# RWKV attention and MLP in one kernel: w spread by a product, the last two tiles turned on TensorE, a new order

## The chip, the cores and the metric

The kernel runs on one core of one Trainium2 chip. The metric is the device time of one execution in microseconds, given as the median of several runs. A core has five engines with a queue of instructions each: TensorE (PE in the profile, with its weight loads as PEld), VectorE (DVE), ScalarE (ACT), GpSimd (POOL) and SyncE (SP), which here only issues DMAs. ACT issues DMAs too. Products of PE land in PSUM and are taken out by DVE or ACT.

## The reference

A recurrence with decay over 768 steps for 4 batches and 8 heads of 48, then a layer norm, a two-layer MLP with relu, and a residual:

```python
for t in range(S):
    cur = np.einsum('bhd,bhe->bhde', u[None] * kt, vt)
    y[:, :, t] = np.einsum('bhd,bhde->bhe', rt, state + cur)
    state = w[None, :, :, None] * state + np.einsum('bhd,bhe->bhde', kt, vt)
...
xn = (x - mu) / np.sqrt(var + 1e-06) * g_ln
ch = np.maximum(xn @ w_ch1, 0.0) @ w_ch2
return x + ch
```

x is y with the heads side by side: 3072 rows of 384. The MLP is 384 to 1536 to 384. Inputs and output are fp32.

## The kernel before

The rows are cut into 24 tiles of 128 steps (tile i is chunk i // 4 of batch i % 4). For each tile, r and k are scaled by powers of w (`SR`, `SK` with the factors `Fr`, `Fk`), turned so that the head dimension lies on partitions (`TR` on PE with copies `TCr`, `TCk`, `TC`; from tile 12 on `TKR`, a DMA transpose issued by SP, into `trs`), multiplied (`Q`), and made into score products (`AT`, masked by `AM` into `A`). `S` makes the state update and the u term in a PSUM bank named s, `CC` and `ZU`/`ZS`/`ZD` take them out, `Y` makes the tile's output in the same bank, and `X` adds the u term `Vb` and sums the row. `CV` casts v to bf16. `SQ`, `XN` and `RS` are the layer norm. xn is then turned again: for the early tiles by `LT` on PE with a copy `XT`, for pairs by `LT2` and for the last four tiles by `LTD`, both DMA transposes on SP, into `xT`.

The MLP goes by groups of one or two tiles (`GROUPS`): `UP` (PE, 12 or 6 products into one of two banks hp), `RL` (relu to bf16 `hT`, ACT or DVE), `DN` (PE, four products each into bank o), `OT` (DVE, scale and residual into one of four slots of `ot`) and `STO` (store). The last tile's output is made in two halves.

Weights come in three slabs for each layer (`LW1`, `LW2`, into the same buffers `w1_f`). `SW` scales each part of a first-layer slab by the layer norm's weight and casts it, `CW` casts the second layer's. The loads of k, r and v (`LK`, `LR`, `LV`) are 192 KB each.

At the start w is loaded to all 128 partitions (`WF`), `LN` takes its logarithm, `FK` and `FR` make the factors. `DU` puts products on a tile of zeros into PSUM that nobody reads (an argument of 8 is two of 512 columns).

Nothing is scheduled by a tool: `PLAN` is a list of steps, each with an index and an engine (s, v, g for ACT, DVE, POOL), and every engine runs its steps in the order of this list. SP carries all loads, the DMA transposes and most stores in one queue, so an issue that waits holds up all that stand behind it.

Of the kernel before, what the change touches and what calls it, by code (L numbers as in the profile page):

```python
# [7 lines left out]
FP32 = mybir.dt.float32  # L8
# [10 lines left out]
WF,0,s LK,0,- MP,0,v MM,0,g LR,0,- MI,0,g MW,0,v LK,1,- LC,0,s DU,8,- TL,0,s DU,16,- LR,1,- LC,1,s DU,48,- LV,0,- LN,0,s LC,2,s FK,0,s LR,2,- FR,0,s  # L19
SK,0,v LK,2,- SR,0,v SK,1,v TR,0,- LV,1,- SR,1,g CT,0,- TCk,0,v DU,8,- LK,3,- CP,0,v CV,0,s UW,0,g TR,1,- TCr,0,s LR,3,- SR,2,v TCk,1,s AT,0,- Q,0,v  # L20
WL,0,s DU,8,- LV,2,- TCr,1,v SK,2,g S,0,- AMb,0,v DU,8,- CC,0,s LV,3,- Q,1,v TR,2,- CV,1,s VB,0,g ZU,0,v DU,8,- TCk,2,s LW1,0,- AMa,0,v S,1,- SK,3,g
TCr,2,s LW1,2,- CC,1,v ZU,1,v AT,1,- UGC,0,s DU,8,- Q,2,g LK,4,- AMa,1,v Y,0,- AT,2,- X,0,v LR,4,- CV,2,g AMa,2,v S,2,- SR,3,g DU,8,- AMb,1,v CC,2,s
CV,3,v VB,1,g TR,3,- ZU,2,v LR,5,- AMb,2,v TCr,3,s Y,1,- XN,0,g DU,8,- SQ,0,s X,1,v DU,8,- TCk,3,s Y,2,- XN,1,g SW,1,s Q,3,v RS,0,g LT,1,- SW,0,v
DU,8,- XT,1,s SW,2,v DU,8,- VB,2,v LT,0,- UP,16,- XT,0,s LV,4,- SW,7,v SW,6,s AT,3,- X,2,v UP,0,- LK,5,- SK,4,v S,3,- RL,16,v RL,0,s LW1,1,- SR,4,g
SW,8,v XN,2,s LR,6,- CC,3,v AM,3,v UP,2,- VB,3,g LK,6,- TR,4,- SR,5,g ZU,3,v UP,18,- TC,4,s LK,7,- LT,2,- SK,5,v Y,3,- RL,2,s Q,4,v TR,5,- X,3,v
DU,8,- CV,4,v XN,3,s S,4,- XT,2,v TC,5,v LR,7,- UP,32,- SW,3,s SW,4,g SW,5,v RL,18,s ATP,4,- Q,5,g ZU,4,v RL,32,s UP,17,- AM,4,v LV,5,- SR,6,g UP,1,-
RL,17,s LV,6,- CC,4,s SQ,1,s RL,1,v Y,4,- VB,4,g UP,33,- SQ,2,s AM,5,v LW2,1,- SK,6,g LT,3,- DU,8,- LW2,0,- XT,3,v TR,6,- LW2,2,- X,4,v DU,2,- UP,49,-
TC,6,s RL,33,v LV,7,- CV,5,v S,5,- SK,7,v SR,7,v UP,50,- ZU,5,v TR,7,- CC,5,v XN,4,v Q,6,v TC,7,s LR,8,- LT,4,- CV,6,v S,6,- RL,50,v XT,4,s Q,7,g
RL,49,s CC,6,v ZU,6,v ATP,6,- CW,3,s UP,34,- VB,5,g AM,6,v CW,2,s Y,5,- RS,2,g LK,9,- DN,5,- CW,0,s CW,1,v RS,1,g X,5,v UP,48,- RL,34,s VB,6,v XN,5,s
Y,6,- DN,4,- RL,48,s X,6,v LR,9,- CW,4,s LT,5,- CW,5,v UP,66,- XN,6,g AM,7,v SQ,3,s DN,6,- UP,64,- LK,11,- OT,1,v CV,7,s S,7,- LK,8,- SR,8,g DN,2,-  # L30
CC,7,s ZU,7,v DN,0,- LR,10,- RL,66,s XT,5,v SK,9,v Y,7,- RL,64,s LV,9,- DN,1,- SR,9,v SQ,5,s VB,7,v UP,80,- LV,8,- OT,0,v TR,9,- X,7,v LR,11,- UP,65,-
SK,8,g TC,9,s DN,8,- LK,10,- RL,65,s Q,9,v TR,8,- SR,10,v RL,80,s LV,10,- DN,10,- CV,9,g XN,7,v SQ,4,s DN,9,- TC,8,s CV,8,g LT2,6,- S,9,- RS,4,g
OT,2,v UP,81,- Q,8,v SR,11,g ATP,8,- LK,12,- ZU,9,v RL,81,s UP,82,- CC,9,v STO,0,s AM,8,v LK,13,- S,8,- SK,10,g RL,82,s DN,18,- LR,12,- ZU,8,v CC,8,s
DN,17,- VB,9,g AM,9,v Y,8,- VB,8,g TR,10,- LV,11,- SK,11,v UP,96,- TC,10,s ZD,8,g X,8,v DN,16,- LV,12,- RL,96,s UP,98,- Q,10,g CV,10,s LR,13,- TR,11,-
XN,8,s Y,9,- SQ,6,s TC,11,v RS,5,g LK,15,- UP,97,- RL,98,s OT,4,v SK,12,g ATP,10,- STO,1,- SQ,7,s X,9,v DN,21,- RL,97,s Q,11,v SR,12,g XN,9,s S,10,-
UP,100,- ZU,10,v RS,3,g TKR,12,- DN,20,- AM,10,v RL,100,s DN,22,- CC,10,s CV,12,s VB,10,g AM,11,v SQ,8,s LV,14,- Y,10,- UP,101,- CV,11,g LT2,8,-
SR,13,g OT,5,v UP,99,- X,10,v DN,13,- LV,13,- RL,99,s ZD,10,v LR,14,- S,11,- RL,101,s ZD,9,v DN,12,- SK,13,v DN,14,- ZU,11,v TKR,13,- UP,112,- Q,12,v
CC,11,v VB,11,v Y,11,- RL,112,s STO,2,- OT,3,v UP,117,- CV,13,v UP,115,- STO,3,- X,11,v SR,14,g LK,14,- DN,29,- XN,11,s LV,15,- Q,13,v RS,6,g S,12,-
RL,117,s ATP,12,- ZU,12,v CC,12,s DN,28,- XN,10,v RL,115,s AM,12,v VB,12,g LT2,10,- DN,30,- ZD,11,g UP,116,- OT,7,v LR,15,- Y,12,- AM,13,v RL,116,s
LK,17,- UP,113,- STO,4,- DN,24,- X,12,v RL,113,s LR,16,- DN,25,- ZD,12,v SK,14,v S,13,- UP,114,- SK,15,v TKR,14,- CC,13,v ZU,13,v UP,133,- VB,13,g  # L40
RL,114,s SR,15,v Y,13,- RL,133,s UP,132,- X,13,v TKR,15,- UP,128,- RL,132,v SR,16,g DN,26,- RL,128,s LK,16,- UP,131,- SQ,9,s OT,6,v CV,14,g LR,17,-
XN,12,s UP,129,- Q,14,v RS,7,g XN,13,s S,14,- DN,32,- CV,15,s ZU,14,v LT2,12,- Q,15,g SQ,13,s ATP,14,- CC,14,v VB,14,v RL,131,s DN,33,- SK,16,g
# [23 lines left out]
def kernel(  # L66
# [12 lines left out]
    nc = tc.nc  # L79
# [87 lines left out]
    w_p = cols[:, :HP]  # L167
# [52 lines left out]
    def MW(i, e):  # L220
        nc.vector.memset(rows[:], 1.0)
        nc.vector.memset(warm[:], 0.0)  # L222
# [433 lines left out]
```

## Time and profile before

| | us |
|---|---|
| median of three runs | 155.81 (155.64 to 156.53) |
| profiled execution | 154.18 |
| its span, first to last instruction | 152.4 |
| PE busy, of it unread products | 141.2, 13.6 |
| DVE, ACT, POOL busy | 113.8, 78.2, 77.7 |
| first up product, first output product | 20.36, 39.67 |

Busy times are unions of an engine's instructions, with the tail of the product pipeline; a product's own mean duration is therefore longer than the distance between two of them. "Idle before" with an arrow names what ended an engine's wait. The chain of waits, followed back from the end, runs mostly over PE (57% of the span) and SP's queue (14%).

### The profile page before, as it was taken

The numbers are of one execution on the slowest core, as the hardware profiler recorded it, in microseconds if no ns is written. First come the engines' busy times: TensorE is split into PE (matmuls) and PEld (weight loads), VectorE is DVE, ScalarE is ACT, GpSimd is POOL, SyncE is SP. The second block draws the span as 40 slices with busy tenths as digits, with TensorE's granted clock in tenths as the row PEclk, the third lists the DMA queues.
The fourth block names the chain that finished last, engine by engine and source line by source line (L and its number), as shares of the span: only waits on it lengthen the run. The fifth ranks groups of instructions, "written<-read, shape, count | busy, mean of one in ns | idle before, by whom it ended". The sixth has DMA issues, their size and how long they took to land.

```text
span 152.4 us, 4296 instructions
## 1 busy us (share of the span) xinstructions
PE 141.2 (93%) x1716; PEld 108.6 (71%) x1716; DVE 113.8 (75%) x238; ACT 78.2 (51%) x169; POOL 77.7 (51%) x115
## 2 busy tenths in 40 slices
PE   4998897899899999999997999799999999999991
PEld 1365477686778878877885788577886776878871
DVE  2449889989777995896976989699869965743521
ACT  1555465666957739635359384411962152934020
POOL 3058836571743979915328948067404909450100
PEclk9999999999999999999999999999999999999999
DMA  3999989999889989689999899988998997133122
GB/s 76 200 230 202 361 180 247 233 232 395 242 165 200 199 197 215 143 174 256 121 228 207 159 216 208 206 172 205 211 217 179 229 200 175 58 96 117 49 103 103
DMA packets 100241, 28.98 MB, mean 190 GB/s; under 512 B 95355, under 2 KB 98686, under 8 KB 100222
## 3 DMA queue, kind: packets, MB, share of 16 engines
q1 hardware_dynamic: 98752, 26.94, 81.0%
q10 hardware_dynamic: 1470, 1.77, 3.4%
q8 instruction: 13, 0.21, 0.6%
q14 instruction: 6, 0.05, 0.1%
HBM read 19.08 MB, written 4.72 MB: 156 GB/s over the span
## 4 chain that ended last, share of the span: by engine, by line
PE 57%; SPq 14%; DMA 11%; POOL 5%; ACT 5%; DVE 3%; issue 3%; POOLq 0%; DVEq 0%; ACTq 0%
PE o L550 23%; PE hp L520 22%; SPq L322 6%; DMA trs<-sc 4%; SPq L319 4%; DMA w_f<-in_moe_w_ch_dram 4%; DMA out_dram<-ot 3%; SPq L325 3%; PE s L437 2%; POOL q L190 2%; PE s L445 2%; PE at L341 2%; PE at L364 2%; POOL sc L190 1%; PE s L408 1%
## 5 line engine op out<-in xcount | busy, mean ns | idle before, releaser
L520 PE MATMUL hp<-xT,w_sb 128*128 128x128 bf16 (+1 forms) x612 | 57.1, 242 | 1.6 <-DVE hT L538 0.6
L550 PE MATMUL o<-w_sb,hT 128*128 128x384 bf16 x276 | 52.2, 326 | 1.5 <-DVE ot L608 1.1
L520 PEld LDWEIGHTS <-w_sb 128*128 128x128 bf16 x612 | 48.6, 114 | 5.6 <-issue 0.7
L536 ACT ACTIVATE hT<-hp 128x512 bf16<-128x512 f32 x56 | 32.9, 597 | 34.4 <-PE hp L520 33.9
L550 PEld LDWEIGHTS <-hT 128*128 128x128 bf16 x276 | 25.1, 97 | 14.5 <-issue 1.7
L374 DVE TENSOR_TENSOR A<-at,mask 128x1024 bf16<-128x1024 f32 (+1 forms) x27 | 29.1, 1094 | 0.0
L608 DVE SCALAR_TENSOR_TENSOR ot<-o,rs,x 128x384 f32<-128x384 f32 x23 | 14.1, 614 | 10.6 <-PE o L550 8.3
L190 POOL TENSOR_TENSOR sc<-rf,Fr 128x384 bf16<-128x384 f32 x12 | 12.4, 1034 | 16.7 <-DMA rf<-in_r_dram 16.7
L427 POOL TENSOR_TENSOR Vb<-vf,cc 128x384 f32<-128x384 f32 x16 | 13.6, 851 | 11.0 <-DVE cc L187 9.6
L257 PE MATMUL o<-warm 128*128 128x512 bf16 x42 | 13.6, 456 | 2.0 <-DVE warm L222 2.0
L452 DVE SCALAR_TENSOR_TENSOR x<-s,Vb 128x384 f32<-128x384 f32 x24 | 13.2, 550 | 2.3 <-PE s L445 1.6
L459 ACT ACTIVATE sqj<-x,sm 128x384 bf16<-128x384 f32 x24 | 14.7, 614 | 0.0
L190 POOL TENSOR_TENSOR q<-trs 128x512 bf16<-128x512 bf16 x8 | 9.2, 1153 | 8.8 <-DMA trs<-sc 4.6
L185 ACT COPY trs<-at 128x512 bf16<-128x512 bf16 (+1 forms) x12 | 9.5, 798 | 8.1 <-PE at L341 6.9
L538 DVE TENSOR_SCALAR hT<-hp 128x512 bf16<-128x512 f32 x16 | 10.8, 685 | 2.5 <-PE hp L520 2.5
L190 DVE TENSOR_TENSOR q<-trs 128x512 bf16<-128x512 bf16 x16 | 8.1, 509 | 4.7 <-DMA trs<-sc 3.3
L190 POOL TENSOR_TENSOR sc<-kf,Fk 128x384 bf16<-128x384 f32 x9 | 9.7, 1082 | 3.8 <-PE o L550 3.2
L190 DVE TENSOR_TENSOR sc<-kf,Fk 128x384 bf16<-128x384 f32 x15 | 8.4, 562 | 4.2 <-ACT Fk L270 4.0
L476 POOL TENSOR_TENSOR rs<-rs,expo 128x1 f32<-128x1 f32 (+1 forms) x17 | 10.7, 632 | 1.4
L465 ACT ACTIVATE xn<-x,sm 128x384 bf16<-128x384 f32 x13 | 7.9, 615 | 5.6 <-DVE x L452 5.6
L473 POOL TENSOR_SCALAR rs<-sq 128x1 f32<-128x1 f32 (+1 forms) x17 | 4.1, 244 | 12.7 <-ACT sqj L459 11.7
L395 PEld LDWEIGHTS <-q 128*128 128x128 bf16 x96 | 5.5, 97 | 4.9 <-DVE q L190 1.3
(75 smaller groups left out, 172.4 us busy)
## 6 DMA issues: line engine op xcount, KB each, us to landing
kf<-in_k_dram SPq DMA_DIRECT2D x24, 192.0 KB, 4.0
rf<-in_r_dram SPq DMA_DIRECT2D x24, 192.0 KB, 3.9
vf<-in_v_dram SPq DMA_DIRECT2D x24, 192.0 KB, 3.8
w_f<-in_moe_w_ch_dram SPq DMA_DIRECT2D x6, 768.0 KB, 7.8
out_dram<-ot SPq DMA_DIRECT2D x16, 192.0 KB, 2.2
out_dram<-ot ACTq DMA_DIRECT2D x7, 192.0 KB, 2.2
w_all<-in_w_dram ACTq DMA_DIRECT2D x1, 192.0 KB, 3.9
trs<-sc SPq DMA_TRANSPOSE x12, 3.6
```

The costliest lines, as they stand in the source:

```text
L190: engines[e].tensor_tensor(out=out, in0=in0, in1=in1, op=ALU.mult)
L257: nc.tensor.matmul(out=warm_ps[0][:], lhsT=warm[:], rhs=warm[:].unsqueeze(1).to_broadcast([P, 4, P]), start=True, stop=True)
L374: nc.vector.tensor_tensor(out=AA(i)[:, a:b].rearrange("p e q t -> p (e q) t"), in0=psum["at", i][:, a:b].rearrange("p e q t -> p (e q) t") ...
L427: engines[e].tensor_tensor(out=Vb(i)[:].rearrange("p (h d) -> p h d", h=H), in0=vf(i)[:], in1=cc(i)[:].unsqueeze(2).to_broadcast([P, H, D] ...
L452: nc.vector.scalar_tensor_tensor(out=xx(i)[:], in0=psum["y", i][:, :C], scalar=1.0, in1=Vb(i)[:], op0=ALU.mult, op1=ALU.add, accum_out=sm[ ...
L459: nc.scalar.activation(out=sqj[:], in_=xx(i)[:], func=ACT.Square, bias=sm[i][:], scale=-float(C), accum_out=sq[g][:, j : j + 1])
L476: nc.gpsimd.tensor_tensor(out=rs[g][:], in0=rs[g][:], in1=expo[:, :n], op=ALU.pow)
L520: nc.tensor.matmul(out=t[:, a * gw : (a + 1) * gw].rearrange("p (j t) -> p j t", j=size), lhsT=w1_sb[n][kc][:, fb::FB], rhs=xT(g)[:, :size ...
L536: nc.scalar.activation(out=o, in_=s, func=ACT.Relu)
L538: nc.vector.tensor_relu(out=o, in_=s)
L550: nc.tensor.matmul(out=psum["o", i][:, :C], lhsT=hT(g)[:, fk, j * P : (j + 1) * P], rhs=w2_sb[d][:, a, :], start=(seen == 0 and a == 0), s ...
L608: nc.vector.scalar_tensor_tensor(out=ot(i), in0=psum["o", i][:, :C], scalar=rs[g][:, j : j + 1], in1=xx(i)[:], op0=ALU.mult, op1=ALU.add,)
```

## The change

Three edits of the code, and a new `PLAN`. w is loaded as one row; a product of a row of ones with it spreads it to 128 partitions in PSUM, in fp32, and `LN` reads it there. The last two tiles' xn is turned by `LT` and `XT` where it was `LTD`. The unread products go from 42 wide and 2 narrow ones to 4 wide ones.

```diff
-    w_all = const.tile([P, H, D], FP32, name="w_all")
+    w_row = const.tile([1, H * D], FP32, name="w_row")
+    one = const.tile([1, P], FP32, name="one")
...
     def WF(i, e):
         issuer(e).dma_start(
-            out=w_all[:].rearrange("p h d -> p (h d)"), in_=w.rearrange("h d -> (h d)").partition_broadcast(P)
+            out=w_row[:], in_=w.rearrange("h d -> (h d)").rearrange("(o x) -> o x", o=1)
         )
...
+        nc.vector.memset(one[:], 1.0)
...
+    def WB(i, e):
+        t = psum["w"] = ps.tile([P, 512], FP32, name="s")
+        nc.tensor.matmul(out=t[:, :C], lhsT=one[:], rhs=w_row[:], start=True, stop=True)
+
     def LN(i, e):
-        nc.scalar.activation(out=ln_all[:], in_=w_all[:], func=ACT.Ln)
+        nc.scalar.activation(
+            out=ln_all[:].rearrange("p h d -> p (h d)"), in_=psum["w"][:, :C], func=ACT.Ln
+        )
...
-WF,0,s LK,0,- MP,0,v MM,0,g LR,0,- MI,0,g MW,0,v LK,1,- LC,0,s DU,8,- TL,0,s DU,16,- LR,1,- LC,1,s DU,48,- LV,0,- LN,0,s LC,2,s FK,0,s LR,2,- FR,0,s
+WF,0,s LR,0,- MP,0,v MI,0,g LK,0,- MW,0,v LC,0,s LC,1,- WB,0,- TL,0,s LV,0,- DU,8,- LR,1,- LK,1,- LC,2,s LN,0,s FR,0,s LR,2,- FK,0,s SR,0,v LK,2,-
```

The sums over engines move too: ACT does 7 fewer casts and scalings of weights, v and xn, POOL 5 more casts of v, 4 more scalings of weights and 5 more scalings of k and r; SP issues 18 full stores where it issued 16.

The first place is SP's queue where the first-layer weight slabs (w1_f) are loaded among tiles of k, r and v (the digit behind kf, rf, vf is the tile). Before:

```order
L319 DMA kf3_72<-in_k_dram 128x8x48
L322 DMA rf3_83<-in_r_dram 128x8x48
L325 DMA vf2_93<-in_v_dram 128x8x48
L325 DMA vf3_94<-in_v_dram 128x8x48
L294 DMA w1_f0_231<-in_moe_w_ch1_dram 128x3x512
L294 DMA w1_f2_233<-in_moe_w_ch1_dram 128x3x512
L319 DMA kf4_73<-in_k_dram 128x8x48
L322 DMA rf4_84<-in_r_dram 128x8x48
L322 DMA rf5_85<-in_r_dram 128x8x48
L325 DMA vf4_95<-in_v_dram 128x8x48
L319 DMA kf5_74<-in_k_dram 128x8x48
L294 DMA w1_f1_232<-in_moe_w_ch1_dram 128x3x512
```

The same place of the changed kernel, after nine rows of tiles 0 to 4:

```order
L332 DMA vf1_92<-in_v_dram 128x8x48
L329 DMA rf3_83<-in_r_dram 128x8x48
L326 DMA kf5_74<-in_k_dram 128x8x48
L326 DMA kf3_72<-in_k_dram 128x8x48
L301 DMA w1_f0_232<-in_moe_w_ch1_dram 128x3x512
L332 DMA vf2_93<-in_v_dram 128x8x48
L326 DMA kf4_73<-in_k_dram 128x8x48
L301 DMA w1_f1_233<-in_moe_w_ch1_dram 128x3x512
L332 DMA vf3_94<-in_v_dram 128x8x48
L329 DMA rf5_85<-in_r_dram 128x8x48
L301 DMA w1_f2_234<-in_moe_w_ch1_dram 128x3x512
```

vf2 and vf3 have moved behind the first and the second slab, and the third slab has come forward past vf4. On PE the first up product (`UP,0`) now stands behind the state products of tile 3 (`S,3`), which read vf3; before, two `UP` stood ahead of `S,3`.

The second place is POOL's queue around the scalings of the first-layer weights (w1_sb, L305 before and L312 now). Before:

```order
L473 TENSOR_SCALAR rs0_198<-sq0_180 128x1
L476 TENSOR_TENSOR rs0_198<-rs0_198,expo_218 128x1
L190 TENSOR_TENSOR sc1_103<-rf4_84,Fr_220 128x8x48
L427 TENSOR_TENSOR Vb0_128<-vf3_94,cc3_119 128x384
L190 TENSOR_TENSOR sc2_104<-rf5_85,Fr_220 128x8x48
L305 TENSOR_SCALAR w1_sb1_1_238<-w1_f1_232,g_neg_228 128x512
L190 TENSOR_TENSOR q1_113<-trs2_111 128x512
```

Now:

```order
L434 TENSOR_TENSOR Vb2_130<-vf2_93,cc2_118 128x384
L312 TENSOR_SCALAR w1_sb0_1_236<-w1_f0_232,g_neg_229 128x512
L312 TENSOR_SCALAR w1_sb1_0_238<-w1_f1_233,g_neg_229 128x512
L190 TENSOR_TENSOR sc2_104<-rf5_85,Fr_220 128x8x48
L312 TENSOR_SCALAR w1_sb1_2_240<-w1_f1_233,g_neg_229 128x512
L312 TENSOR_SCALAR w1_sb2_2_243<-w1_f2_234,g_neg_229 128x512
L187 CAST vv2_107<-vf6_97 128x384
L312 TENSOR_SCALAR w1_sb2_0_241<-w1_f2_234,g_neg_229 128x512
L190 TENSOR_TENSOR sc0_102<-rf6_86,Fr_220 128x8x48
```

POOL scaled one part of nine before and scales five now, with the cast of vf6 between the third slab's two parts.

More of the change, by code (lines that the diff above doesn't have):

```diff
@@ new lines @@
+LV,6,- SW,3,g X,2,v CV,3,s LT,1,- SK,5,v XN,2,s LK,6,- S,3,- AM,3,v SR,5,g SQ,1,s UP,0,- SW,5,g XT,1,v ZU,3,v UP,16,- CC,3,v VB,3,v LT,2,- SW,4,v
+TR,5,- RL,16,s XT,2,v Y,3,- RL,0,s LK,7,- DU,8,- SW,8,g X,3,v UP,33,- Q,4,v LV,5,- CV,4,s XN,3,v S,4,- TC,5,s SW,7,v LR,7,- CV,6,g LT,3,- UP,32,-
+XT,3,v RL,33,s SW,6,g Q,5,v LR,6,- ATP,4,- RL,32,s SK,6,v UP,34,- LW2,0,- AM,4,v UP,18,- LW2,1,- RL,34,s CC,4,v UP,17,- RL,18,s ZU,4,v VB,4,v LW2,2,-
+Y,4,- RL,17,s CV,5,v UP,1,- SR,7,v LV,7,- UP,50,- RL,1,s X,4,v SR,6,g AM,5,v SQ,4,s S,5,- SQ,2,s RS,1,g LR,9,- TR,6,- ZU,5,v RL,50,s UP,2,- RS,0,g
@@ new lines @@
+SK,13,g DN,20,- SK,12,v SR,13,g Y,10,- OT,5,v TKR,12,- UP,96,- X,10,v DN,14,- RS,3,g AM,11,v XN,10,s TKR,13,- DN,12,- CV,11,g RL,98,s DN,13,- SQ,8,s
+Q,11,v SR,14,v LK,14,- S,11,- RL,96,s OT,3,v UP,117,- LV,14,- ZD,9,v DN,28,- STO,3,- RL,117,s CC,11,v CV,13,v VB,11,g UP,112,- ZU,11,v LR,15,- CV,12,s
+Q,12,v Y,11,- ZD,10,g LV,15,- RL,112,s UP,113,- X,11,v SQ,9,s UP,115,- Q,13,g SQ,11,s ATP,12,- STO,4,- RL,115,v XN,11,s S,12,- SK,14,g STO,2,-
+RL,113,s AM,12,v DN,29,- LT2,10,- DN,30,- CV,14,g CC,12,v ZU,12,v SK,15,g UP,116,- OT,7,v TKR,14,- Y,12,- VB,12,v SR,15,g DN,25,- X,12,v DN,24,-
@@ new lines @@
+VB,15,v UP,146,- LR,18,- OT,9,v UP,147,- LK,19,- RL,146,s DN,42,- CV,16,s RL,147,v Q,16,g DN,41,- X,15,v UP,145,- XN,14,v XN,15,s S,16,- RL,145,s
+LT2,14,- DN,40,- ZU,16,v SQ,13,s UP,144,- OT,10,v LV,17,- UP,149,- SK,18,v RL,144,s STO,9,- CC,16,v Q,17,v ATP,16,- VB,16,g RL,149,s LR,19,- DN,46,-
+STO,7,s AM,16,v LV,18,- SR,18,g SQ,14,s DN,45,- UP,163,- AM,17,v RS,9,g TKR,18,- Y,16,- RL,163,s CV,17,g UP,161,- ZD,15,v SK,19,g LR,21,- UP,165,-
+X,16,v RL,161,s DN,44,- RL,165,s SR,19,v S,17,- XN,16,s UP,148,- TKR,19,- CC,17,v OT,11,v VB,17,g UP,162,- ZU,17,v RL,148,s ZD,16,v Q,18,g DN,52,-
@@ new lines @@
+LV,19,- CV,18,s SQ,15,s LK,21,- Y,17,- DN,53,- X,17,v SR,21,g UP,160,- RL,162,v XN,17,s S,18,- RS,10,g RL,160,s LT2,16,- DN,54,- ZU,18,v SQ,17,s
+ATP,18,- CC,18,v OT,13,v VB,18,g SQ,16,s STO,8,- UP,164,- ZD,17,v ZD,18,g LR,20,- DN,48,- AM,18,v RL,164,s LK,20,- DN,50,- STO,10,- SK,21,g AM,19,v
+DN,49,- Y,18,- UP,177,- OT,12,v TKR,21,- X,18,v UP,181,- RL,177,s Q,19,v DN,56,- CV,19,s STO,11,- SK,20,v S,19,- LK,23,- DN,58,- CC,19,s ZU,19,v
+RL,181,s LK,22,- DN,57,- SR,20,v UP,179,- TKR,20,- OT,14,v Y,19,- Q,21,v RL,179,s DN,60,- VB,19,v LR,22,- XN,18,v UP,178,- X,19,v LV,20,- UP,180,-
@@ L62 @@
+DN,90,- RL,256,s DN,88,- STO,21,s DN,89,- DB,1,- OT,22,v DB,0,- DB,2,- STO,22,- DA,1,- OB,23,v DA,0,- SB,23,- DA,2,- OA,23,v SA,23,s
 """
@@ L617 @@
     steps = dict(
-        WF=WF, LC=LC, CT=CT, CP=CP, LT2=LT2, TKR=TKR, DU=DU, MW=MW, TL=TL, MI=MI, MM=MM, MP=MP, WU=WU, LN=LN, FK=FK_, FR=FR_, UGC=UGC,
+        WF=WF, WB=WB, LC=LC, CT=CT, CP=CP, LT2=LT2, TKR=TKR, DU=DU, MW=MW, TL=TL, MI=MI, MM=MM, MP=MP, WU=WU, LN=LN, FK=FK_, FR=FR_, UGC=UGC,
         UW=UW, WL=WL, LW1=LW1, SW=SW, LW2=LW2, CW=CW, LK=LK, LR=LR, LV=LV, SK=SK, SR=SR, CV=CV, TR=TR, TCr=TCr,
```

66 lines of the change are left out of this document (24 added, 42 removed).

## The prediction

> **What bounds the kernel now.** I read the page first, then the busy times by stretch, the waits of TensorE in its timeline, and the waits for loads in the first 40 us.
>
> ```profile
> PE 141.2 (93%) x1716; PEld 108.6 (71%) x1716; DVE 113.8 (75%) x238; ACT 78.2 (51%) x169; POOL 77.7 (51%) x115
> ...
> PEclk9999999999999999999999999999999999999999
> DMA  3999989999889989689999899988998997133122
> ```
>
> TensorE (PE) is busy for 93% of the span, and the DMA engines are full up to the slice that ends at 126 us. Both could be the bound. The stretches decide:
>
> ```profile
> 35.00:40.00 5.00, 4.37 (x76) 3.38 (x74) 5.00 (x13) 3.73 (x6) 2.40 (x4) 1.00 1.01 382
> ...
> 80.00:90.00 10.00, 9.11 (x112) 7.26 (x110) 7.94 (x15) 7.19 (x18) 7.85 (x9) 1.00 0.98 194
> 90.00:100.00 10.00, 8.94 (x100) 6.91 (x97) 8.64 (x19) 4.69 (x11) 4.48 (x7) 1.00 0.99 201
> ...
> 120.00:130.00 10.00, 9.68 (x111) 7.35 (x109) 7.20 (x14) 4.36 (x12) 5.46 (x7) 1.00 0.82 184
> ```
>
> In the second column PE misses 0.89, 1.06 and 0.32 us in these three stretches; in the other stretches between 40 and 140 us it misses 0.20 together. So from 40 us on PE sets the end, and 2.47 us of waiting is all that a better order could take out there. Between 35 and 40 us VectorE (DVE, fourth column) is busy for 5.00 of 5.00: there it is VectorE that holds PE back. The three waits are:
>
> ```profile
> 81.29 0.77 DVE L190 TENSOR_TENSOR q<-trs 128x512 bf16<-128x512 bf16 x1 [0.78 <-DMA trs<-sc]
> 82.11 0.25 PE L395 MATMUL s<-uwI,q 128*128 128x2 bf16 x4 [0.89 <-DVE q L190]
> ...
> 98.05 0.62 DVE L608 SCALAR_TENSOR_TENSOR ot<-o,rs,x 128x384 f32<-128x384 f32 x1 [1.35 <-DMA out_dram<-ot]
> 98.72 0.48 PE L550 MATMUL o<-w_sb,hT 128*128 128x384 bf16 x2 [1.06 <-DVE ot L608]
> ...
> 126.84 0.25 PE L395 MATMUL s<-uwI,q 128*128 128x2 bf16 x4 [0.32 <-POOL q L190]
> ```
>
> The first and third wait for a DMA transpose (through q), the second for a store that must leave its slot of ot. The chain of waits gives that store 4.05 us, and the table of issues gives the transposes 3.6 and 2.9 us:
>
> ```profile
> 93.87 4.05 DMA out_dram<-ot
> ...
> trs<-sc SPq DMA_TRANSPOSE x12, 3.6
> xT<-xn SPq DMA_TRANSPOSE x11, 2.9
> ```
>
> **The unread products and the clock.** The products on warm are read by nobody:
>
> ```profile
> L257 PE MATMUL o<-warm 128*128 128x512 bf16 x42 | 13.6, 456 | 2.0 <-DVE warm L222 2.0
> ...
> 1.95 6.75 PE L257 MATMUL o<-warm 128*128 128x512 bf16 x18 [1.95 <-DVE warm L222]
> ...
> 6.62 0.15 PEld L257 LDWEIGHTS <-warm 128*128 128x128 bf16 x1 [0.28 <-issue]
> 7.05 0.15 PEld L257 LDWEIGHTS <-warm 128*128 128x128 bf16 x1 [0.28 <-issue]
> 7.46 0.75 PEld L257 LDWEIGHTS <-warm 128*128 128x128 bf16 x4 [0.26 <-issue]
> ```
>
> One started every 0.43 us until 7.46, and then four loads took 0.75 us, about half. The granted clock says 9 in every slice, so this slow start shows in the spacing alone: it lasted 5.5 us from the first product at 1.95 on, under unbroken work. Taking out 38 wide and both narrow ones gives back no PE time by itself, since nearly all of them stand in the first 36 us in gaps where PE waits for loads. What it may cost is that slow start at a worse place.
>
> **The loads of the opening.**
>
> ```profile
> 3.11 1.28 ACT L225 ACT_TABLE_LOAD   x1 [3.11 <-issue]
> 4.60 0.52 ACT L267 ACTIVATE ln_all<-w_all 128x384 f32<-128x384 f32 x1 [0.20 <-DMA w_all<-in_w_dram]
> 8.14 1.00 POOL L190 TENSOR_TENSOR sc<-rf,Fr 128x384 bf16<-128x384 f32 x1 [6.01 <-DMA rf<-in_r_dram]
> 10.76 1.00 POOL L190 TENSOR_TENSOR sc<-kf,Fk 128x384 bf16<-128x384 f32 x1 [0.33 <-DMA kf<-in_k_dram]
> 20.36 0.83 PE L520 MATMUL hp<-xT,w_sb 128*128 128x128 bf16 x12
> 21.22 0.49 DVE L303 TENSOR_SCALAR w_sb<-w_f,g_neg 128x512 bf16<-128x512 f32 x1 [0.52 <-DMA w_f<-in_moe_w_ch_dram]
> 28.40 0.72 ACT L301 ACTIVATE w_sb<-w_f,g_neg 128x512 bf16<-128x512 f32 x1 [0.64 <-DMA w_f<-in_moe_w_ch_dram]
> 29.66 1.50 PE L520 MATMUL hp<-xT,w_sb 128*128 128x128 bf16 x24 [0.54 <-ACT hT L536]
> 32.45 0.59 PE L257 MATMUL o<-warm 128*128 128x512 bf16 x2
> 33.57 0.27 PE L261 MATMUL o<-warm 128*128 128x128 bf16 x2
> 39.67 0.81 PE L550 MATMUL o<-w_sb,hT 128*128 128x384 bf16 x4 [0.39 <-ACT w_sb L185]
> ```
>
> rf1 landed at 8.14 and kf2, three transfers later on SP, at 10.76: 0.87 us for one 192 KB load. Two weight slabs were in by 21.22, the third came at 28.40 after five loads: 28.40 - 21.22 - 5 x 0.87 = 2.83 us for a slab. Ahead of the third slab stood 17 loads and the 192 KB of w_all. Now 16 loads stand there and w is one row: two loads less, so the third slab lands at 28.40 - 2 x 0.87 = 26.7.
>
> The first up product, however, now stands behind the state product of tile 3 on PE, and that needs vf3, which has moved behind two slabs: 15 loads and two slabs, where 13 (w_all counted) and two made 21.22. So 21.22 + 2 x 0.87 = 23.0, a cast of 0.5 and the products of 0.3: first up product at 23.8 (before: 20.36). Until it reaches the third slab PE has, by the rows below, four up groups (2.68), the transposes of tile 5 (0.45), scores of two tiles (0.55), two turns of xn (0.34), two unread products (0.43) and about 0.67 of small ones: 5.1 us, to 28.9 at full clock.
>
> ```profile
> 32.44 0.17 PE at L505 x3
> ...
> 43.01 0.65 PE o L550 x4
> 43.66 0.67 PE hp L520 x12
> ...
> 47.85 0.45 PE at L341 x8
> ...
> 59.96 0.55 PE at L364 x16
> ...
> L187 POOL CAST vv<-vf 128x384 bf16<-128x384 f32 x7 | 3.9, 554 | 2.9 <-DMA vf<-in_v_dram 2.8
> L305 POOL TENSOR_SCALAR w_sb<-w_f,g_neg 128x512 bf16<-128x512 f32 x1 | 1.0, 972 | 2.7 <-DMA w_f<-in_moe_w_ch_dram 2.7
> ```
>
> GpSimd scales two of the third slab's three parts, and the cast of vf6 stands between them; vf6 lands at 26.7 + 2 x 0.87 = 28.4. So 28.4 + 0.55 + 0.97 = 29.9: that, not the slab, lets PE go on.
>
> Before had done the same PE work (one up group less, one turn more) at 29.66 - 0.67 + 0.17 = 29.2. If the slow clock were over by 23.8, the change stands at 29.9, 0.7 behind; with 3.5 us of it at 30.6 (28.9 + 1.75), 1.4 behind; with the 5.5 us seen above at 31.7, 2.5 behind. I take 3.5 us: some transposes and scores run before 23.8, but far thinner than the unread products were.
>
> From 29.66 to the first output product at 39.67 before had 10.0 us for about 7.3 us of work: 2.7 lost, VectorE being full and the unread products holding 0.9. The change takes two scalings off VectorE there, has its second weights 1.7 us earlier and none of these products; its loss lies between 0.8 and 2.7, and I take 1.5, since a full VectorE remains likely. That is 1.2 us better. **Opening: +1.4 - 1.2 = +0.2 us**, bounds -1.2 (full clock, 0.8 lost) and +2.5.
>
> The fp32 product that spreads w isn't in this trace. [...] ln_all can't start before the table load ends at about 4.4 anyway, and what hangs on it waits for vf3 at 23.0: I take 0. [...]
>
> **From 40 us on.** I added up PE work by these row durations between an issue and its use, over the two orders. From the transposes of r and k (tiles 12 to 23) to the score products before has 4.7 us on average, the change 5.6; from xT's transpose to the first up product (tiles 12 to 19) before has 2.5 to 3.5, the change 3.7 to 4.8, against landings of 3.6 and 2.9. In the 50 us of PE work in the middle VectorE's instructions sum to 51.3 us before and 48.0 after; GpSimd's rise from 28 to 35, still under 50. So both transpose waits (0.89, 0.32) should go, and part of the store wait. **I take 1.7 of the 2.47 us: -1.7**, bounds -2.5 and +2.0 (as many new waits of 1 us as are removed, and two more).
>
> **The last two tiles.** Six more turns on PE, 2 x 0.17 = **+0.34 us**; PE is full there, so all of it counts. The two DMA transposes that go take nothing from PE: the timeline shows no PE wait after 126.84. The tail behind the last product (two halves and their stores) is unchanged: 0.
>
> Sum: 0.2 - 1.7 + 0.34 = -1.2 us on a span of 152.4, whose execution took 154.18; the median shown is 155.81, 1.6 above it, and I set the sum against that: **154.6 us**.
>
> **The rivals.**
>
> A, slow clock: all 5.5 us fall on the up products and later tiles start late, so that the waits of 2.47 stay. Opening +1.3 (2.5 - 1.2), turns +0.34: 157.4, slower. For it: between 14 and 23 us PE waits for vf2, kf4 and vf3 with few products in between. Against: four tiles of scores do run there. It decides once slow running passes about 5 us. [...]
>
> B, moved, not removed: waits come back elsewhere at two thirds of their size; 155.81 + 0.2 + 0.34 - 0.8 = 155.6, no change. For it: the DMA engines stay full to 126 us and no load of k, r or v is saved.
>
> C, stores: SP now issues 18 of 23 full stores (16 before, rows below), behind transposes that wait. Slots of ot come round with 2.6 to 3.2 us of PE work at tiles 16 to 18, as for tile 10, the wait at 98.72. Three such waits of 1.06: 154.6 + 3.2 = 157.8; one is 155.7. It decides from two waits on. Against: these fall after 120 us, where a store lands in 2.2.
>
> ```profile
> out_dram<-ot SPq DMA_DIRECT2D x16, 192.0 KB, 2.2
> out_dram<-ot ACTq DMA_DIRECT2D x7, 192.0 KB, 2.2
> ```
>
> **How the numbers follow.** Forecast 0.49, A 0.20, B 0.16, C 0.15. A measurement here tells 0.5% (0.78 us) from no change, so faster is below 155.03 (the forecast), slower above 156.59 (A and C): 0.49, 0.16, 0.35. The likeliest's own range is 153.0 to 155.0; with the bounds of the opening and the rivals, less the far ends, 152.8 to 157.5.
>
> **What would show it.** Right: third slab's scaling near 27 us, first up product near 24, first output product near 39, under 1 us of PE idle between 40 and 140 us. Wrong: up groups of 12 taking 1.3 us beyond 28 us (A); a wait of an output product for ot from tile 16 on (C); PE waiting for q or xT in the middle (B); a first output product after 41 us.

## The result and the profile after

The changed kernel took 155.28 us (median of 20 runs, 152.44 to 158.16) where the kernel before took 156.13 (20 runs, 154.18 to 158.64): ratio 0.989, 95% interval 0.986 to 0.993. It is faster by about half a per cent; the forecast of 154.6 us was 0.7 too low.

Two things must be known before any number below is read. Runs of one kernel spread over 3 to 4%, so the differences in this document are differences of means over all runs, and the figure behind +- is twice the standard error (for six runs a 95% interval is up to a quarter wider). The printed ratios leave out runs over 1.5% above a kernel's lowest, so they hang on its one or two lowest; in three sets of the change they read 0.989, 1.000 (0.996 to 1.004) and 0.993. And a profile is one run: that of the kernel before, on which the prediction was built, was the shortest of its 20 (154.18), while that of the change is an ordinary one (155.74). So the kernel before was profiled twice and the change three times; each edited kernel below has one profile.

The page of the change, first part and the issues:

```profile
PE 138.6 (90%) x1684; PEld 109.8 (71%) x1684; DVE 116.7 (76%) x243; ACT 72.7 (47%) x156; POOL 84.2 (55%) x126
...
out_dram<-ot SPq DMA_DIRECT2D x18, 192.0 KB, 3.1
...
trs<-sc SPq DMA_TRANSPOSE x12, 4.4
xT<-xn SPq DMA_TRANSPOSE x9, 3.4
```

TensorE lost 2.6 us of busy time although most of 13.6 us of unread products went: they had stood in gaps. VectorE and GpSimd have more to do, ScalarE less. The DMA transposes land later than the 3.6 and 2.9 us of before (3.2 and 3.2 in the second profile of that kernel; 4.1 to 4.4 and 3.3 to 3.5 in the three of the change).

The timeline of the change in the opening (start, duration, engine, what it waited for):

```profile
2.27 1.61 PE L269 MATMUL s<-w_row,one 1*128 1x384 f32 x2 [2.27 <-DMA w_row<-in_w_dram]
3.92 0.49 ACT L272 ACTIVATE ln_all<-s 128x384 f32<-128x384 f32 x1
24.11 2.76 PE L527 MATMUL hp<-xT,w_sb 128*128 128x128 bf16 x24
27.56 0.69 POOL L312 TENSOR_SCALAR w_sb<-w_f,g_neg 128x512 bf16<-128x512 f32 x1 [1.72 <-DMA w_f<-in_moe_w_ch_dram]
28.88 0.83 PE L527 MATMUL hp<-xT,w_sb 128*128 128x128 bf16 x12
39.12 0.81 PE L557 MATMUL o<-w_sb,hT 128*128 128x384 bf16 x4
```

The opening went as forecast: first up product at 24.11 (forecast 23.8), third slab at 27.56 (near 27), first output product at 39.12 (near 39). In the two other profiles of the change these times are 24.12 and 23.68, 26.36 and 26.03, 39.02 and 39.30. The first two up groups ran at about half speed (2.76 us for 24 products, against 0.83 for the 12 at 28.88).

The middle did not. The same stretches as before, and the one between 110 and 120 us:

```profile
80.00:90.00 10.00, 9.28 (x118) 7.01 (x117) 7.62 (x15) 4.34 (x10) 9.18 (x11) 1.00 1.18 206
90.00:100.00 10.00, 9.96 (x108) 8.11 (x105) 8.39 (x16) 5.72 (x12) 5.18 (x7) 1.00 0.91 199
...
110.00:120.00 10.00, 9.27 (x99) 7.07 (x97) 7.91 (x18) 3.50 (x9) 2.80 (x4) 1.00 0.91 192
120.00:130.00 10.00, 9.41 (x119) 7.76 (x117) 7.69 (x17) 4.66 (x11) 4.47 (x9) 1.00 1.02 190
```

Between 40 and 140 us TensorE (second column) misses 2.70 us in all; it was 2.47 before. The old wait for a store at 98.7 is gone in all three profiles of the change, and others stand in its place; the two largest of the last third, which the other two profiles have too (0.44 and 0.45, 0.68 and 0.73 us), are

```profile
119.40 1.46 PE L557 MATMUL o<-w_sb,hT 128*128 128x384 bf16 x8 [0.47 <-DVE ot L615]
...
127.30 0.40 PE L371 MATMUL at<-trs 48*128 48x128 bf16 x8 [0.59 <-DMA trs<-sc]
```

The chain of waits, which ran over TensorE for 57% of the span in the first profile before, runs over it for 36% here:

```profile
PE 36%; DVE 15%; DMA 14%; POOL 13%; SPq 11%; issue 7%; ACT 2%; POOLq 0%; DVEq 0%
```

Nothing can be built on that: the second profile of the kernel before has 34%, and the other two of the change 49 and 36%.

The following account is used throughout. All columns are read from the timelines and from stretches: start of the first output product, TensorE's idle time from there to 140 us, start of the last group of score products (`at<-trs`), span; the last two columns are differences of these.

| profile | first output | idle | last scores | span | span - last scores | span - first output - idle |
|---|---|---|---|---|---|---|
| before | 39.67 | 2.47 | 127.02 | 152.4 | 25.4 | 110.3 |
| before, again | 40.67 | 2.75 | 128.26 | 153.6 | 25.3 | 110.2 |
| change | 39.12 | 2.77 | 127.30 | 154.0 | 26.7 | 112.1 |
| change, again | 39.02 | 2.43 | 126.45 | 153.1 | 26.7 | 111.7 |
| change, third | 39.30 | 2.31 | 126.78 | 153.4 | 26.6 | 111.8 |

Two constants come out. Behind the last score products the timelines of all five profiles show no wait of TensorE (it is busy for 10.00 of the 10 us from 130 on in each), so the span ends a fixed time later: 25.3 us in the old order, 26.6 in the new. And what stands behind TensorE's first output product is 1.6 us more in the new order (111.85 against 110.22 on the means): the first output product comes about 1 us earlier, but with less done ahead of it (361 product records against 392, unread products and the one that spreads w left out). From 40 to 140 us the idle times are 2.47 and 3.14 us before and 2.70, 2.36 and 2.31 with the change.

### The profile page after: what moved, and what is told of

The parts are those of the page before. It is cut to its first block, busy times and chain, and to the rows that moved or that the text cites. A ratio compares the mean times of both kernels' runs of the same rounds, so it can differ in the third digit from the quotient of the medians.

```text
span 154.0 us, 4244 instructions
## 1 busy us (share of the span) xinstructions
PE 138.6 (90%) x1684; PEld 109.8 (71%) x1684; DVE 116.7 (76%) x243; ACT 72.7 (47%) x156; POOL 84.2 (55%) x126
## 4 chain that ended last, share of the span: by engine, by line
PE 36%; DVE 15%; DMA 14%; POOL 13%; SPq 11%; issue 7%; ACT 2%; POOLq 0%; DVEq 0%
PE o L557 15%; PE hp L527 14%; DMA trs<-sc 6%; DMA kf<-in_k_dram 5%; DVE A L381 4%; POOL sc L190 3%; SPq L326 3%; DMA vf<-in_v_dram 3%; SPq L301 3%; SPq L329 2%; POOL Vb L434 2%; DVE sc L190 2%; DVE w_sb L187 2%; PE s L452 2%; POOL q L190 1%
## 5 line engine op out<-in xcount | busy, mean ns | idle before, releaser
L527 PEld LDWEIGHTS <-w_sb 128*128 128x128 bf16 x612 | 49.7, 115 | 4.5 <-issue 1.1
L190 POOL TENSOR_TENSOR sc<-rf,Fr 128x384 bf16<-128x384 f32 x15 | 15.7, 1047 | 11.9 <-DMA rf<-in_r_dram 11.9
L474 POOL TENSOR_SCALAR xn<-x,sm 128x384 bf16<-128x384 f32 x8 | 6.0, 749 | 17.7 <-DVE x L459 17.4
L190 POOL TENSOR_TENSOR sc<-kf,Fk 128x384 bf16<-128x384 f32 x11 | 11.0, 999 | 2.5 <-DMA trs<-sc 1.7
L472 ACT ACTIVATE xn<-x,sm 128x384 bf16<-128x384 f32 x11 | 6.8, 615 | 11.8 <-DVE x L459 11.8
L348 PE MATMUL at<-ident,sc 128*128 128x128 bf16 x96 | 10.0, 264 | 2.2 <-DVE sc L190 1.2
L452 PE MATMUL s<-vv,A 128*128 128x48 bf16 x192 | 9.4, 189 | 2.3 <-DVE cc L187 1.0
L185 ACT COPY trs<-at 128x512 bf16<-128x512 bf16 (+1 forms) x11 | 7.9, 740 | 6.6 <-PE at L348 6.1
L190 POOL TENSOR_TENSOR q<-trs 128x512 bf16<-128x512 bf16 x7 | 8.1, 1157 | 5.3 <-DMA trs<-sc 5.3
L348 PEld LDWEIGHTS <-sc 128*128 128x128 bf16 x96 | 7.5, 118 | 4.5 <-DVE sc L190 2.7
```

The costliest lines, as they stand in the source:

```text
L190: engines[e].tensor_tensor(out=out, in0=in0, in1=in1, op=ALU.mult)
L348: nc.tensor.transpose(out=t[:, a * HP + q, :], in_=flat[:, q, :], identity=ident[:])
L452: nc.tensor.matmul(out=t[:, h * D : (h + 1) * D], lhsT=AA(i)[:, par, q, :], rhs=vv(i)[:, h, :], start=first, stop=True, skip_group_check=True,
L527: nc.tensor.matmul(out=t[:, a * gw : (a + 1) * gw].rearrange("p (j t) -> p j t", j=size), lhsT=w1_sb[n][kc][:, fb::FB], rhs=xT(g)[:, :size ...
```

## The experiments

**Both kernels again.** No edit.

> The kernel before, unchanged, for a second profile of it and as a measure of what two equal kernels differ by. Single executions of each kernel spread over some 4 us, and the profile that the prediction was made from was one of the shortest. If that execution was short because its transfers landed early, this profile is longer (span 153.5 to 155) and has more than 2.47 us of PE idle between 40 and 140 us, with transposes and stores that take longer than 3.6 and 2.2 us to land. If the spread is outside the kernel's span, the span is again 152.4 and the idle time again about 2.5. Time against before: 1.00 within 0.5%.

> The changed kernel, unchanged, for a second profile. Time against before: 0.985 to 0.994. If the gain sits in the part from 40 us on (theory of the prediction), PE idle between 40 and 140 us is smaller here than in the second profile of before, by 1 to 2 us. If it sits in the opening (rival), idle there is equal and the first output product of this profile stands earlier for the same PE work.

Measured on one chip: before 155.73 us (median of 12), the change 154.87; difference of means -0.71 +- 0.50 us. Against all 35 runs of the kernel before on that chip, the change stands at -0.81 +- 0.55. The second profile of the kernel before has its waits elsewhere, and more of them:

```profile
67.08 0.81 PE L550 MATMUL o<-w_sb,hT 128*128 128x384 bf16 x4 [1.24 <-DVE ot L608]
99.93 1.46 PE L550 MATMUL o<-w_sb,hT 128*128 128x384 bf16 x8 [1.07 <-DVE ot L608]
```

The wait of 0.89 us for a transpose at 82.1, on which a part of the forecast rested, is down to nothing here, and one of 1.24 stands at 67; the wait for the store's slot (1.06 at 98.7 before) is there again. So some waits in the middle belong to the run and some to the order. The transposes of r and k landed no later (3.2 us), against the expectation. The second profile of the change has 0.8 us less idle time from 40 to 140 us than this one, and its first output product stands 1.65 us earlier: a part of each theory, and neither alone.

**Thirty unread products in the gaps of the opening.**

```diff
-WB,0,- ... DU,8,- ... CT,0,- ... TR,1,- ... AT,1,- ... S,1,- ... TR,2,- ... TR,3,- ... S,2,- ... TR,4,- ... DU,8,-
+WB,0,- DU,24,- ... CT,0,- DU,8,- ... TR,1,- DU,8,- ... AT,1,- DU,8,- ... S,1,- DU,16,- ... TR,2,- DU,8,- ... TR,3,- DU,32,- ... S,2,- DU,8,- ... TR,4,- DU,8,-
```

> The changed kernel with unread products put back into the gaps of the opening (30 wide ones before the first up product, none after it), nothing else changed. They are no part of the computation. If the slow start of the clock costs what the prediction charged (1.75 us of PE time), the first two up groups take 0.7 us each where they took 1.4, and the kernel is 0.8 to 1.6 us faster than the changed one (0.995 to 0.990 of it). If the casts and scalings bound the opening anyway (VectorE full from 20 to 40 us, GpSimd's last scaling of the third slab), the up groups run fast but the first output product stays within 0.5 us of 39.1 and the time is the same within 0.3 us. If the unread products delay the early chains, it is slower by 0.5 or more.

The up products ran at full clock from the first, and the first output product came at 38.24 us (39.02 to 39.30 with the change):

```profile
23.95 0.83 PE L527 MATMUL hp<-xT,w_sb 128*128 128x128 bf16 x12
```

The time did not move: 155.04 us on the mean, 0.03 +- 0.70 from the change. In the profile, which is of one of its longer runs (156.13), the 0.8 us won in the opening were gone by the last scores (127.48), which had no wait of their own; TensorE had waited 1.42 us for xT at 89.6. In the new order the slow clock is real and costs nothing that could be measured.

**w by DMA to all partitions again,** the product that spreads it taken out.

```diff
-            out=w_row[:], in_=w.rearrange("h d -> (h d)").rearrange("(o x) -> o x", o=1)
+            out=w_all[:].rearrange("p h d -> p (h d)"), in_=w.rearrange("h d -> (h d)").partition_broadcast(P)
...
-LC,1,- WB,0,- TL,0,s
+LC,1,- TL,0,s
```

> The changed kernel with w loaded to all 128 partitions by DMA again and the fp32 product taken out; order otherwise kept. If the opening is set by the transfers, as the prediction has it, every landing from the second load on is 0.87 us later and the kernel is 0.5 to 0.9 us slower than the changed one. If the opening's end is set by the engines, the landings are later by the same amount but the time is the same within 0.3 us.

Everything in the opening came 1.2 to 1.4 us later than on the mean of the change's three profiles: first up product at 25.22, third slab at 27.84, first output product at 40.57. The last scores stood at 127.79, and the mean was 0.80 +- 0.84 us above the change. The 0.87 us of one 192 KB transfer, the forecast's estimate from the landings before, fit that, but the difference is at the limit of what was measured.

**The last two tiles' transposes on the DMA queue again.**

```diff
-XN,22,g ... LT,22,- ... XT,22,v ... XN,23,g ... LT,23,- ... XT,23,s
+XN,22,g LTD,22,- ... XN,23,g LTD,23,-
```

> The changed kernel with xn of tiles 22 and 23 transposed by DMA again, as before the change, so that six turns of 0.17 us leave TensorE and two transposes go back to the queue; all else stays. If TensorE is full there and the transposes are hidden (my term of +0.34 us was real), the time falls by 0.3 us, to 154.6 to 154.7. Rival: the product waits for the transposed xn, since the order gives it less distance (a landing takes 2.2 to 3.4 us): then the trace shows TensorE waiting for xT after 130 us, and the time stays or rises by up to 1 us.

It ran on a second chip, with the kernels that follow; the kernel before takes 154.4 us there (29 runs in each of two sets, 154.46 and 154.43 on the mean). The mean was 156.46 us: 1.99 +- 0.90 above the kernel before, and 2.32 +- 1.03 above the change as measured there below. The rival's sign was right, but the place was another: TensorE waited for xT at 79.7 (0.91), yet not after 130; it waited for ot. The profile is of a run of 158.32 us, 1.9 above the mean, and its first output product stands at 40.11, 1.0 us late, ahead of all that the edit touches. SP's queue, then VectorE and TensorE:

```profile
129.60 5.54 SPq L487 DMA_TRANSPOSE xT<-xn  x2
135.24 5.34 SPq L622 DMA_DIRECT2D out_dram<-ot  x3
```

```profile
139.60 0.62 DVE L615 SCALAR_TENSOR_TENSOR ot<-o,rs,x 128x384 f32<-128x384 f32 x1 [2.51 <-DMA out_dram<-ot]
```

```profile
140.27 1.46 PE L557 MATMUL o<-w_sb,hT 128*128 128x384 bf16 x8 [1.53 <-DVE ot L615]
```

The transpose of tile 22 stands on SP until xn is ready (133.9), the stores behind it start at 135.24, their slot of ot comes free at 139.6, and an output product is 1.53 us late. The edit puts each transpose right behind its xn on SP, ahead of these stores; another place for it was not tried. The 1.53 us are the part of the loss that the profile ties to the edit.

**No unread products, in the new and in the old order.** In the old order all `DU` steps go, 42 wide products and 2 narrow ones (not 54, as the expectation has it).

```diff
-DU,8,- ... DU,8,-
```

> The changed kernel without its two times eight unread products. If the slow start of TensorE costs nothing at the end (30 early unread products moved the total by nothing against this kernel), the time stays within 0.4 us of the changed kernel's 155.0 and the second output of the trace, the first output product, stays between 38.5 and 39.5 us. Rival, slow clock: without any work in the gaps TensorE runs slower for longer, the first output product comes after 40 us, and the time rises by 1 us or more.

> The kernel before without any of its 54 unread products, all else the same. If they only fill gaps and the slow start does no harm (theory of no effect), the time stays within 0.4 us of before, or falls by the 0.9 us that the unread products at 32.45 and 33.57 us hold. Rival, slow clock: the slow start of about 5 us falls on the up products from 20.4 us on, and the time rises by 1 to 2.5 us.

The new order: 154.65 us on the mean, 0.52 +- 0.86 from the change. The first output product came at 37.73, 1.4 us earlier and before either expectation, although its first 24 up products took 2.69 us; the idle time from 40 to 140 us rose to 3.17 and the last scores stood at 126.46, so that again the gain of the opening was spent before the end.

The old order: 157.76 us, 3.30 +- 0.58 above the kernel before. The slow start shows, though the granted clock reads 1.00 in all of this opening:

```profile
20.89 1.44 PE L520 MATMUL hp<-xT,w_sb 128*128 128x128 bf16 x12 [0.25 <-ACT xT L185]
22.80 1.47 PE L520 MATMUL hp<-xT,w_sb 128*128 128x128 bf16 x12
24.50 0.85 PE L520 MATMUL hp<-xT,w_sb 128*128 128x128 bf16 x12
```

Two groups lose 0.6 us each, but the first output product stands at 40.28, between the two profiles of the kernel before. The loss lies behind it, even in this profile, which is of the shortest of its six runs (156.66): 4.56 us idle, nearly all for transposes or what hangs on them, as at

```profile
92.64 0.24 PE L395 MATMUL s<-uwI,q 128*128 128x2 bf16 x4 [0.79 <-DVE x L452]
...
129.49 0.25 PE L395 MATMUL s<-uwI,q 128*128 128x2 bf16 x4 [0.91 <-POOL q L190]
```

So, by this profile, the clock rival is wrong in its path even where the size fits it: the slow start cost the first output product nothing.

**Only the first 18 unread products kept in the old order.**

```diff
 DU,8,- ... DU,16,- ... DU,48,-
-DU,8,- (twelve times) ... DU,2,-
```

> The kernel before with only its first 18 unread products (up to 8.7 us), the other 24 wide and 2 narrow ones out. Without any of them it took 3.3 us more. If the slow start was what these 3.3 us were made of, the first 18 are enough to end it, and the time goes back to within 0.5 us of the kernel before. If the later ones matter, because they hold TensorE's place in the order or keep the clock up in the gaps of 10 to 21 us, the time stays 2 us or more above.

155.59 us, 1.15 +- 0.49 above the kernel before: between the two expectations. This run shows a fall of TensorE's clock in the record of the granted clock (column ahead of the last two):

```profile
10.00:11.00 1.00, 0.53 (x15) 0.36 (x14) 1.00 (x4) 0.96 (x4) 0.25 (x1) 1.00 1.13 222
11.00:12.00 1.00, 0.71 (x14) 0.54 (x11) 1.00 (x4) 0.86 (x3) 1.00 (x2) 0.90 1.07 209
12.00:13.00 1.00, 0.86 (x12) 0.62 (x10) 1.00 (x3) 0.71 (x3) 1.00 (x2) 0.50 1.10 216
...
24.00:25.00 1.00, 1.00 (x16) 1.00 (x14) 0.49 (x2) 0.92 (x2) 0.25 (x1) 0.50 1.20 238
25.00:26.00 1.00, 1.00 (x17) 1.00 (x15) 1.00 (x2) 0.18 (x1) 1.00 (x2) 0.77 0.85 215
26.00:27.00 1.00, 1.00 (x26) 1.00 (x24) 0.97 (x2) 0.84 (x1) 0.56 (x1) 1.00 0.99 385
```

The unread work ends near 7.5 us, the clock falls to 0.50 within the twelfth microsecond and stays there until about 25.5, five microseconds after the up products began at 20.66. Three up groups ran at 1.40 to 1.47 us. Its first output product stood at 40.08 all the same, and its waits (2.99 us idle) are those of the kernel without any, some smaller and one (0.98 at 117.0) gone.

**w as one row in the old order.**

```diff
-LC,0,s DU,8,- TL,0,s DU,16,-
+LC,0,s WB,0,- DU,8,- TL,0,s DU,16,-
```

> The kernel before with one part of the change alone: w comes as one row of 1.5 KB and is spread by one fp32 product ahead of the first unread ones, so that 192 KB leave the head of the transfers. If the opening hangs on the order in which transfers land (undoing this part in the changed kernel cost 0.8 us), the third slab's scaling moves from 28.4 to 29.4 us down by about 0.9 us, and the time falls by 0.5 to 0.9 us against the kernel before. Rival: VectorE, full between 35 and 40 us, holds the first output products at 39.7 to 40.7 us whenever the slab lands: then the time stays within 0.3 us.

155.21 us, 0.75 +- 0.72 above the kernel before, so neither theory's number. The timeline shows a gain and a loss in the opening:

```profile
2.15 1.61 PE L270 MATMUL s<-w_row,one 1*128 1x384 f32 x2 [2.15 <-DVE one L224]
3.69 6.42 PE L259 MATMUL o<-warm 128*128 128x512 bf16 x18
```

The product takes 1.61 us, the 18 unread ones begin at 3.69 where they began at 1.95, and the first score product behind them comes at 11.79 instead of 10.38. The transfer's gain is there: the third slab's scaling begins at 27.56, and at 28.40 and 29.40 in the two profiles of the kernel before. But the first output product stands at 40.46, between the two of that kernel, and like theirs it waits 0.39 us for a cast on ScalarE. So the slab's landing doesn't set it; what the 0.75 us are made of, this profile (of a run of 154.47, 0.7 below the mean) doesn't show.

**The change a third time, the waits taken out of its order, and stores moved to ScalarE.** The edits of the second and the third kernel:

```diff
-DU,8,- (twice)
-Q,20,v ... OT,15,v
+OT,15,v Q,20,v
-Y,15,- ... UP,146,-
+UP,146,- Y,15,-
-ATP,22,- ... DN,64,-
+DN,64,- ATP,22,-
```

```diff
-STO,8,- ... STO,10,- ... STO,11,- ... STO,13,-
+STO,8,s ... STO,10,s ... STO,11,s ... STO,13,s
```

> The changed kernel once more, unchanged, as the yardstick for the three beside it. The end follows the landing of the last scores' transposes: in five profiles of kernels in the new order TensorE waits 0.6 to 1.0 us for it at 126.4 to 127.8 us, and the span ends 26.4 to 26.8 us later. Expected again: a wait of 0.5 to 1.0 us near 127, span 26.6 us after it, time 0.3 to 0.6% below the kernel before.

> The changed kernel with four small moves: its unread products out, the eviction of tile 15's output ahead of the scaled q of tile 20 on VectorE (a wait of 0.45 us near 118.5), the product of tile 15's A and v one up group later (a wait of 0.46 near 88.7), and the last score products one output group later on TensorE, behind work that needs no transpose (the wait of 0.6 to 1.0 us near 127). If the last transposes alone set the end, the 0.65 us of output work that now runs during that wait comes off the time and the other two moves give nothing: -0.6 us against the changed kernel. If TensorE's own work sets the end, all three waits come off: -1.5 us. Rival: the waits come back elsewhere, 0.

> The changed kernel with four stores (tiles 8, 10, 11 and 13) issued by ScalarE instead of SP, no other instruction moved. In the profile SP issues almost without a gap from 103 to 128 us, 0.58 us for a load or a store and 1.2 us or more for a transpose. If SP's issuing sets when the last transposes land, these come about 1 to 1.5 us earlier (at 125 to 126 instead of 126.4 to 127.3) and the time falls by up to 1 us. Rival, the DMA engines are full whoever issues: the landing stays and the time moves by less than 0.3 us. Third: ScalarE's own work comes late behind its issues, and the time rises by 0.3 to 1 us.

The change: 154.13 us on the mean, -0.30 +- 0.63 against the kernel before; ratio 0.993, 0.989 to 0.998.

The reordered kernel: 153.69 us, -0.74 +- 0.96 against the kernel before by means (six runs), ratio 0.989 with an interval of 0.983 to 0.995; against the change -0.44 +- 1.10. It is the lowest mean and has the shortest profile of the study, with a span of 151.1 us (of a run 0.8 below its mean). The three waits are gone or smaller (others of 0.41 and 0.42 us stand at 79.5 and 80.3), the idle time is 1.63 us, and span minus last scores is 26.0 where the change has 26.6: the 0.65 us of one output group. The last wait that is left:

```profile
125.06 0.40 PE L371 MATMUL at<-trs 48*128 48x128 bf16 x8 [0.31 <-DMA trs<-sc]
```

The mean fits the first theory's 0.6 us, but six runs exclude neither nothing nor 1.5; that the kernel beats the change is not settled.

Stores on ScalarE: 154.46 us, 0.33 +- 0.74 above the change, which leaves the two other expectations open. SP came to the last two transposes at 118.50, 1.6 to 2.6 us earlier than in the change, but stood on them for 4.12 us. The last scores waited longer, 1.11 us, and stood at 126.40, so the theory that SP's issuing sets them falls. What does set them is read from the rows ahead of them, here of the change a third time:

```profile
115.72 0.56 DVE L190 TENSOR_TENSOR sc<-kf,Fk 128x384 bf16<-128x384 f32 x1 [0.87 <-DMA kf<-in_k_dram]
116.89 1.00 POOL L190 TENSOR_TENSOR sc<-kf,Fk 128x384 bf16<-128x384 f32 x1 [1.35 <-DMA trs<-sc]
118.11 1.00 POOL L190 TENSOR_TENSOR sc<-rf,Fr 128x384 bf16<-128x384 f32 x1 [0.23 <-DMA rf<-in_r_dram]
118.62 2.34 DVE L381 TENSOR_TENSOR A<-at,mask 128x1024 bf16<-128x1024 f32 x2
120.29 3.10 SPq L497 DMA_TRANSPOSE trs<-sc  x2
121.54 0.55 DVE L190 TENSOR_TENSOR sc<-rf,Fr 128x384 bf16<-128x384 f32 x1
```

The last two transposes are those of tiles 22 and 23; each needs its tile's scaled k and r. GpSimd scales k of tile 23 at 116.89, when an earlier transpose has left its slot of sc (there are three), and r of tile 22 at 118.11. VectorE, which has no gap from 115.72 on, when a load of k has landed, comes to r of tile 23 last, at 121.54, behind 2.34 us of masking. SP's row ends 1.3 us after that scaling (also in the two other profiles of the change and in the kernel with stores on ScalarE), and the scores follow 3.4 us later. By these rows the last scores hang on VectorE's order rather than on SP or on a slot of sc, and for some 11 us, from 115.7 to 126.8, TensorE's lead counts for nothing. This is a reading of the trace and no test; the scaling of that r further forward on VectorE would be one, and wasn't tried.

## Why the prediction was right, and where not

**Opening, +0.2: right in sum.** The three times came within 0.9 us of the forecast's. In the account, the first output product is 1.0 us earlier (39.15 on the mean of three, 40.17 on the mean of two), and 1.6 us more stands behind it; less the 0.34 of the turns that is 1.3, so the opening is 0.3 worse. Forecast 0.2, with bounds of -1.2 and +2.5. The parts fit less well than the sum: TensorE came to the third slab at 31.3 to 31.5, where the forecast had 30.6.

**From 40 us on, -1.7: this step failed in size.** The forecast left under 1 us of idle time; the three profiles of the change have 2.3 to 2.7 us. Against 2.8 on the mean of the two before that is 0.3 instead of 1.7. The step compared distances in the order with landings of 3.6 and 2.9 us, read from one run. Of the waits that it counted, the one for the store's slot went in every profile, and the one at 82.1 was missing in the second profile of the old order as well. But the landings rose to 4.1 to 4.4 and 3.3 to 3.5, which may have taken up the distance won (no run separates that), and waits that no transpose makes came up behind: for ot near 119 in all three profiles, for Z near 89 in two; the third waits 0.80 us for xT at 79.4. Rival B described this.

**Turns, +0.34: the work is there, but the alternative was mis-sized.** The forecast let the two DMA transposes go at no gain. In the new order putting them back cost 2.3 +- 1.0 us, of which the profile shows 1.53, by way of the stores behind them on SP. That is rival C's path, which in the change itself made one wait of 0.44 to 0.47 us for ot, not three of 1.06.

**Slow clock: right.** I took 3.5 us of half clock from the first up product, a choice between none and the 5.5 us of the trace before, which doesn't show how long it would last there. In the first profile it lasted over 4 us, to between 28.2 and 28.9, since the transposes at 26.99 still took 1.06 us for 8 (0.61 at 35.84) and the unread products at 28.19 0.85 us for 2; in the two others it lasted some 3 to 4 us (8 transposes in 0.86 us at 27.01 in the second, 2 unread products in 0.59 us at 27.75 in the third). Rival A needed 5 us of it to decide. It would have been wrong in the time even so: the kernel with thirty early unread products had none of it, and ended no earlier (0.03 +- 0.70). In the kernel with 18 early unread products the granted clock fell to 0.50 near 11.8 us, some 4 us after them; TensorE had been busy for 0.25 to 0.71 of each microsecond from 8 to 12. And it stayed at 0.50 until about 25.5, with TensorE busy for 3.14, 2.39 and 3.75 us of the 4 us from 12, 16 and 20 on: in this run the clock fell under the one stretch of thin work and stayed low under the other, into the up products that begin at 20.66.

**The product that spreads w: right at 0, though it took 1.61 us.** It runs at the slow start (the two unread products behind it take 1.03 us, against 0.59 at 32.45 before), under the table load, which ends at 3.91, and ln_all comes at 3.92 instead of 4.60.

**The sum, -1.2:** measured -0.93 +- 0.79, -0.71 +- 0.50 and -0.30 +- 0.63 us in three sets. What the forecast has too much is in the term of 1.7, and that the time came so near in spite of it is in part luck. What brings the gain is not settled by the profiles: by their spans the change would be 0.5 us longer (153.5 against 153.0). Both profiles of the kernel before were among its shorter runs (154.18 and 155.39, with means of 156.12 and 155.72), while the three of the change lie 0.5 us above its means on average. So what an ordinary run of the old order loses, and the new one doesn't, no profile here shows; it may be idle time in the middle after all. Two parts of the change cost something when they were undone: the turns (2.3 +- 1.0, with the transposes in one place of SP's queue) and, at the limit, w as a row (0.8 +- 0.84). In the old order w as a row won nothing, so these are no shares of the gain.

## What to carry to other kernels

In this order, with TensorE busy for 90% of the span, VectorE for 76% and SP's queue for 23.9 of the 26.3 us from 102.84 on, an earlier opening didn't reach the end by itself: with the first output product at 38.24 and 37.73 instead of 39.15 the time was 0.03 +- 0.70 and 0.52 +- 0.86 us above the change. A place to look is the last wait that every profile of the kernel shows, here that for the last transposed scores, and work that doesn't need it can be put in front; here that took 0.6 us off the part behind it, and its effect on the time is not settled. Taking one part out of an order that was searched with it tells what the part is worth in that order alone: without unread products the old order lost 3.3 us and the new one nothing that could be measured. And profile the kernel before twice, since a sum of waits from one run may be made of waits that the next run doesn't have.

## What the hardware showed that was not expected

The record of the granted clock shows a fall, but not a slow start: it read 1.00 in the old order without unread products, while up groups took 1.44 us instead of 0.85, and 0.50 for 14 us with the first 18 of them kept, where 8 transposes took 0.61 us at 7.33, ahead of the fall, and 1.01 at 16.63.

The same transposes, issued at the same place of the old order, took longer in one kernel than in the other. The kernel before, SP's row and that of the first reader:

```profile
85.30 3.06 SPq L490 DMA_TRANSPOSE trs<-sc  x2
```

```profile
89.51 0.48 DVE L190 TENSOR_TENSOR q<-trs 128x512 bf16<-128x512 bf16 x1 [0.71 <-DMA trs<-sc]
```

and without unread products:

```profile
85.66 3.15 SPq L490 DMA_TRANSPOSE trs<-sc  x2
```

```profile
91.22 0.42 DVE L190 TENSOR_TENSOR q<-trs 128x512 bf16<-128x512 bf16 x1 [2.06 <-DMA trs<-sc]
```

That is 4.2 us from the issue to the reader in the one and 5.6 in the other. It is no chance of one run: the second profile of the kernel before has 4.0, and the kernel with the first 18 unread products has 5.6 (85.56 to 91.19). Nothing in these queues was edited; the cause stays open, and with it most of the 3.3 us.

Two chips differed by 1.4 us on the kernel before (155.8 and 154.4 on the mean), more than this change is worth. Times were compared only within one chip; of the profiles in the account, the third of the change is from the second chip.
